# A gated convolution and two MLPs: VectorE's share per unit, block 2's softmax and convolution, and the order inside Y

## The chip, the cores and the metric

The kernel runs on one core of one Trainium2 chip. The metric is the device time of one execution in microseconds (us). The engines are TensorE (PE, with its weight loads listed as PEld), VectorE (DVE), ScalarE (ACT), GpSimd (POOL) and SyncE (SP), which issues the DMAs.

## What is computed

```python
# x: 2 x 4096 x 192, weight_gen: 2 x 4096 x 8 heads x 7 taps; 8192 tokens in all
w = softmax(weight_gen, axis=-1)
out = causal convolution of x with 7 taps, weights w per token and head   # 8192 x 192
xn = out / sqrt(mean(out * out) + 1e-6) * rms_g
g = xn @ w_gate                      # 192 x 1536
x = (g * sigmoid(g) * (xn @ w_val)) @ w_out       # 1536 x 192
h = x @ w_in                         # 192 x 2048
return (h * sigmoid(1.702 * h)) @ w_out2          # 2048 x 192
```

The weight matrices arrive as floats of 64 bits and are split ("decoded") on the chip into a high and a low part; everything else is of 32 bits.

## The kernel before

The 8192 tokens are 16 blocks of 512. Every matmul has a moving operand of 512 tokens and uses 64 of the 128 rows, so they go in pairs, one on the upper rows and one on the lower. Each factor is held as a high part in the reduced format fp32r and a low part, the difference; products are sums of high x high, low x high and high x low.

The work on PE is a list of units. A unit of kind 1, written (1, b, m), makes the gate and value sums of one of 12 column tiles of block b (U1, PSUM tiles pg and pv). A unit of kind 2, (2, b, i), makes two of the 16 column tiles of the second MLP (U2, two tiles ph). Into each unit are woven the down matmuls of earlier units (D1 two units later, D2 one unit later for blocks 0 and 1 and mostly two later else), which add into the long-lived sums a and b. A unit of kind 1 with its down has 14 pairs, one of kind 2 with two has 19. The list begins with 24 units of kind 1, blocks 0 and 1 mixed (unit 6 is (1,1,2), unit 23 is (1,1,11)), then 16 of kind 2, blocks 0 and 1 mixed (24 is (2,0,0), 28 is (2,1,0), 29 is (2,0,4), 36 is (2,1,4)), and unit 40 is (1,2,0). From block 2 on the order repeats: the rest of block b's kind 1, four units of kind 1 of block b + 1, the eight of kind 2 of block b.

Behind the matmuls of a kind-1 unit ACT writes p = silu(pg) (L485), DVE multiplies p by pv (L489), ACT copies p to h (L490), DVE writes l = p - h (L493). In kind 2 ACT makes two silus for each tile, h and p (L506, L507), and DVE l (L513). The PSUM pool of pg, pv and ph has four buffers, so a unit's two tiles are those of two units before: PE's first pair of unit i + 2, which writes both, waits until DVE's p (or ACT's silu) of unit i has read them.

Y(b) (L526), behind the unit with block b's last D1, turns the sums a and b of the first MLP into the inputs of the second: ACT copies two halves of b into yt crosswise (L537, L538) and a into yh (L539); DVE adds b to yt (L540), writes yl = a - yh (L541); ACT copies yt to ysh (L542); DVE writes ysl = yt - ysh (L543).

Weights come in 34 pieces of 384 columns, loaded three ahead. A piece is decoded by one multiply on ACT (x1, L95), five DVE steps (L99, L103, L107, L111, L117) and one or two ACT casts (x6, L122); `piece_steps` runs these for three pieces at once, so that DVE's five steps stand together. Softmax and convolution (softmax_ops, conv_ops) are DVE steps too, but for the exp (ACT, L188, which needs another ACT table than silu), the squares (ACT, L273), the inverse root (POOL, L278 and L280) and half of the scaling (`sc`, DVE L284, ACT L287). In blocks 0 to 4 PE transposes the result.

Every engine runs its instructions in the order in which they are written. A small planner sets that order: stream 0 holds the piece steps and stream 1 softmax and convolution steps, each with a cost and the unit by which it must be done. `share(k, i)` gives the credit that stream k gets in unit i to meet the tightest due unit, and `some` spends it, half ahead of `second` (p and h) and half between `second` and `third` (l); up to unit (1,1,2) both halves stand behind. `ex_at` is the unit at whose head the exp is written, `xt_at` the unit in which a block's transposes are. When a PSUM bank goes from matmuls of the upper rows to matmuls of the lower, a word from POOL (`handed`, L395) stands between.

Of the kernel before, what the change touches and what calls it, by code (L numbers as in the profile page):

```python
# [9 lines left out]
F32 = mybir.dt.float32  # L10
# [8 lines left out]
P = 128  # L19
# [23 lines left out]
def gated_conv_mlp(ctx: ExitStack, tc: tile.TileContext, xp, wg, w1, wo1, w2, wo2, g, out):  # L43
# [174 lines left out]
    def conv_ops(b):  # L218
# [64 lines left out]
        def sc(j):  # L283
            nc.vector.tensor_scalar_mul(out=xr[:, j, 0:D], in0=acc_of[j], scalar1=ri[:, j:j + 1])  # L284
            if b >= TURN:
                return
            nc.scalar.mul(out=xr[:, j, D:2 * P], in_=acc_of[j][:, P:D], mul=ri[:, j:j + 1])  # L287
        for j in range(T):
            ops.append((230, lambda j=j: sc(j)))
        xrow[b] = xr  # L290
# [235 lines left out]
    def Y(b):  # L526
        N = BLOCKS[b] * P
        pa, pb = acc1.pop(b)
        g = "0" if b in (0, NB - 1) else ""
        W = N if g else NM  # L530
        h = ytp.tile([P, W], F32R, tag="yh" + g, name=f"yh{b}")
        l = ytp.tile([P, W], F32R, tag="yl" + g, name=f"yl{b}")
        sh = ytp.tile([P, W], F32R, tag="ysh" + g, name=f"ysh{b}")
        sl = ytp.tile([P, W], F32R, tag="ysl" + g, name=f"ysl{b}")
        t = zp.tile([P, NM], F32, tag="zb", name=f"yt{b}")

        nc.scalar.copy(t[0:DR, :N], pb[DR:P, :N])  # L537
        nc.scalar.copy(t[DR:P, :N], pb[0:DR, :N])  # L538
        nc.scalar.copy(h[:, :N], pa[:, :N])  # L539
        nc.vector.tensor_tensor(out=t[:, :N], in0=t[:, :N], in1=pb[:, :N], op=ALU.add)  # L540
        nc.vector.tensor_tensor(out=l[:, :N], in0=pa[:, :N], in1=h[:, :N].bitcast(F32), op=ALU.subtract)  # L541
        nc.scalar.copy(sh[:, :N], t[:, :N])  # L542
        nc.vector.tensor_tensor(out=sl[:, :N], in0=t[:, :N], in1=sh[:, :N].bitcast(F32), op=ALU.subtract)  # L543
        yT[b] = (h, l, sh, sl)

    def Z(b, own=None):
        N = BLOCKS[b] * P
# [44 lines left out]
        xt_at[b] = pos[1, b - 1, M1 - 8 if b >= TURN else M1 - 2]  # L592
    xt_by_pos = {v: k for k, v in xt_at.items()}
    splits = {}
    group_of = {b0: gi for gi, (b0, b1) in enumerate(GROUPS)}


    at = [0.0]
    for kind, b, m in units:
        at.append(at[-1] + (14 if kind == 1 else 19) * 0.454 * BLOCKS[b] * P)  # L600


    need = []
# [49 lines left out]
    def share(k, i):  # L653

        total, rate = 0.0, 0.0
        for end, c, _ in streams[k]:
            total += c
            rate = max(rate, total / max(1.0, at[min(end, len(units))] - at[i]))
        return rate * (at[i + 1] - at[i])

    def some(amounts):
        for k, a in enumerate(amounts):
# [16 lines left out]
    with ExitStack() as order:  # L679
# [42 lines left out]
        run(conv1[TAPS + 2:])  # L722
        sm[2] = softmax_load(2)
        for p, _ in need[1:]:
            add_work(0, max(0, p - LOOK), [(2150, piece_steps)])
        nxt = 2
        ex_hook = None
        start_at = pos[1, 1, 2]
        soft = {}
        for i, u in enumerate(units):  # L730
            kind, b, m = u
            if (kind, b, m) == (1, 2, 0):
                early.close()
                late = ctx.enter_context(tc.tile_pool(name="late", bufs=6))
                parts.append((late, late))
                squares.append(ctx.enter_context(tc.tile_pool(name="squares", bufs=1)))
# [13 lines left out]
            if i == start_at:  # L750
                if nxt < 4:
                    load_x(nxt)
                end = xt_at[nxt]
                gi = group_of.get(nxt)
                if gi in soft:
                    add_work(1, end - 2, soft.pop(gi) + conv_ops(nxt))
                elif gi is not None and gi >= 2:
                    pr, ex_hook, post_ops = softmax_ops(gi, sm[gi])
                    ex_at = i + 4 if gi == 2 else pos[2, nxt - 2, 2]
                    add_work(1, ex_at, pr)  # L760
                else:
                    gi = group_of.get(nxt + 1)
                    if gi is not None and gi >= 4:
                        pr, ex_hook, soft[gi] = softmax_ops(gi, sm[gi])
                        ex_at = pos[2, nxt - 2, 2]
                        add_work(1, ex_at, pr)
                    add_work(1, end - 2, conv_ops(nxt))
                gi = group_of.get(nxt + (1 if nxt < 4 else 2))
                if gi is not None and gi >= 2 and gi not in sm:
                    sm[gi] = softmax_load(gi)  # L770
# [9 lines left out]
                downs.append(d)  # L780
                after += [f] if f else []
            second, third = (U1 if kind == 1 else U2)(b, m, lambda *ups: matmuls(ups, downs, kind == 2 and b < 2))
            todo = [share(k, i) / 2 for k in (0, 1)]
            if i == 0:
                split = transpose_x(1)
                split(dves=False)
                second()
                split(acts=False)
                third()
                some(todo)  # L790
                some(todo)
            elif i < pos[1, 1, 2]:
                second()
                some(todo)
                third()
                some(todo)
            else:
                some(todo)
                second()
                some(todo)  # L800
                third()
# [60 lines left out]
```

## Time and profile before

| | us |
|---|---|
| median of three runs | 1241.3 (1240.44 to 1241.46) |
| profiled execution | 1240.54 |
| its span | 1238.6 |

The span runs from the first to the last instruction of the profiled execution; 1.9 us lie around it. A row of a timeline has the start, the duration, the engine and line, the operation with its output and inputs, and in brackets the idle time of the engine ahead of it with what ended that. Durations of neighbours overlap a little, so the distance of two starts is the cost in a queue. PE and PEld are one engine: weight loads run beside the matmul before them.

### The profile page before, as it was taken

How to read it: one execution, taken by the hardware profiler on the slowest of the kernel's cores; microseconds unless marked ns; L12 is line 12 of the kernel's file. 1: busy time of each engine (PE TensorE's matmuls, PEld its weight loads, DVE VectorE, ACT ScalarE, POOL GpSimd, SP SyncE). 2: the span in 40 equal slices, each digit the busy share in tenths (PEclk: the TensorE clock that was granted, in tenths of full speed). 3: DMA queues.
4: the chain of work that ended last, by engine and by line, in shares of the span. 5: the costliest groups of instructions: out<-in, count | busy, mean ns of one | idle time of the engine just before them, and what ended most of it. 6: DMA issues, size and time to landing. Idle time of an engine off the chain costs nothing.

```text
span 1238.6 us, 26868 instructions
## 1 busy us (share of the span) xinstructions
PE 1215.7 (98%) x10324; PEld 1100.3 (89%) x10324; DVE 773.1 (62%) x1296; ACT 650.2 (52%) x1279; POOL 32.3 (3%) x53
## 2 busy tenths in 40 slices
PE   5999999999999999999999999999999999999998
PEld 3776999988888999999999989999899998888897
DVE  8989847576657475665747557475664746545432
ACT  4666664555646445454564545446454554544553
POOL 4000000000000000000000000000000000000000
PEclk9999999999999999999999999999999999999999
DMA  5865411001101000110001001001100011000000
GB/s 187 274 182 185 133 57 46 2 1 58 33 16 48 7 25 33 42 34 11 21 33 31 33 16 59 7 26 33 31 33 11 22 33 31 1 15 18 1 14 13
DMA packets 33855, 57.51 MB, mean 46 GB/s; under 512 B 7744, under 2 KB 19392, under 8 KB 33728
## 3 DMA queue, kind: packets, MB, share of 16 engines
q1 hardware_dynamic: 33728, 55.80, 14.5%
q8 instruction: 81, 1.33, 0.4%
q14 instruction: 46, 0.38, 0.1%
HBM read 43.71 MB, written 6.29 MB: 40 GB/s over the span
## 4 chain that ended last, share of the span: by engine, by line
PE 90%; DVE 7%; ACT 2%; issue 1%; DMA 0%; POOL 0%; DVEq 0%; POOLq 0%; ACTq 0%
PE a L380 24%; PE ph L380 21%; PE b L380 16%; PE pv L380 14%; PE pg L380 14%; DVE p L489 1%; DVE l L493 1%; DVE xr L229 1%; DVE dec_a L107 1%; ACT h L490 0%; DVE w L117 0%; DVE dec_s L99 0%; DVE dec_s L111 0%; DVE o L117 0%; DVE acc L262 0%
## 5 line engine op out<-in xcount | busy, mean ns | idle before, releaser
L380 PE MATMUL a<-h,o 64*128 64x512 f32 x1788 | 517.0, 391 | 0.0
L380 PEld LDWEIGHTS a<-h,o 64*128 64x128 f32 x1788 | 326.7, 184 | 14.2
L513 DVE TENSOR_TENSOR l<-p,h 128x512 fp32r<-128x512 f32 x256 | 176.1, 691 | 235.2 <-ACT p L507 233.6
L380 PE MATMUL b<-l,o 64*128 64x512 f32 x896 | 311.2, 393 | 0.1
L380 PE MATMUL a<-l,o 64*128 64x512 f32 x894 | 310.0, 392 | 1.0 <-DVE l L513 0.8
L380 PE MATMUL b<-h,o 64*128 64x512 f32 x896 | 310.4, 392 | 0.0
L506 ACT ACTIVATE h<-ph 128x512 fp32r<-128x512 f32 x256 | 153.9, 601 | 208.5 <-PE ph L380 199.9
L380 PE MATMUL pv<-xh,w 64*128 64x512 f32 x768 | 241.9, 394 | 1.6 <-DVE p L489 1.1
L380 PE MATMUL pg<-xh,w 64*128 64x512 f32 x768 | 242.0, 393 | 1.2 <-ACT w L122 1.2
L380 PE MATMUL ph<-yh,w 64*128 64x512 f32 x1024 | 234.4, 392 | 1.6 <-DVE p L489 1.4
L490 ACT CAST h<-p 128x512 fp32r<-128x512 f32 x192 | 119.4, 622 | 186.3 <-DVE p L489 186.3
L485 ACT ACTIVATE p<-pg 128x512 f32<-128x512 f32 x192 | 114.6, 597 | 164.3 <-PE pg L380 163.7
L489 DVE TENSOR_TENSOR p<-p,pv 128x512 f32<-128x512 f32 x192 | 131.6, 685 | 104.1 <-PE a L380 72.3
L493 DVE TENSOR_TENSOR l<-p,h 128x512 fp32r<-128x512 f32 x192 | 132.6, 691 | 82.9 <-ACT h L490 82.6
L380 PEld LDWEIGHTS a<-l,o 64*128 64x128 f32 x894 | 165.1, 185 | 14.3 <-DVE l L513 2.5
L380 PEld LDWEIGHTS b<-l,o 64*128 64x128 f32 x896 | 165.5, 185 | 8.7 <-DVE l L493 0.5
L380 PEld LDWEIGHTS b<-h,o 64*128 64x128 f32 x896 | 163.9, 185 | 7.7 <-POOLq L395 0.5
L380 PEld LDWEIGHTS ph<-yh,w 64*128 64x128 f32 x1024 | 145.3, 185 | 15.1 <-DVE p L489 2.1
L507 ACT ACTIVATE p<-ph 128x512 f32<-128x512 f32 x256 | 153.9, 601 | 0.0
L380 PEld LDWEIGHTS pv<-xh,w 64*128 64x128 f32 x768 | 140.8, 185 | 14.3 <-DVE p L489 3.8
L380 PE MATMUL ph<-yl,w 64*128 64x512 f32 x512 | 151.2, 391 | 0.0
L380 PE MATMUL pv<-xl,w 64*128 64x512 f32 x384 | 150.5, 392 | 0.0
(117 smaller groups left out, 2098.2 us busy)
## 6 DMA issues: line engine op xcount, KB each, us to landing
x<-in_xp SPq DMA_DIRECT2D x15, 960.0 KB, 4.8
st<-in_w SPq DMA_DIRECT2D x20, 384.0 KB, 4.0
zt<-in_w SPq DMA_DIRECT2D x20, 384.0 KB, 3.4
st<-in_wo SPq DMA_DIRECT2D x14, 384.0 KB, 3.9
zt<-in_wo SPq DMA_DIRECT2D x14, 384.0 KB, 3.4
out_z<-za SPq DMA_DIRECT2D x16, 256.0 KB, 2.2
xl<-raw SPq DMA_DIRECT2D x176, 16.0 KB, 1.8
xsl<-raw SPq DMA_DIRECT2D x176, 16.0 KB, 1.8
```

The source lines that it names most:

```text
L107: nc.vector.scalar_tensor_tensor(out=ai, in0=ai, scalar=3, in1=t["s"], op0=ALU.logical_shift_left, op1=ALU.bitwise_or)
L229: eng.tensor_tensor(out=dst.rearrange("p (q g) -> p q g", g=GRP), in0=x[:, (k + j0) * D:(k + j1) * D].rearrange("p (q g) -> p q g", g=GRP) ...
L380: ins = nc.tensor.matmul(ps[:, :N], w[rows], x[rows, :N], start=start, stop=stop)
L485: nc.scalar.activation(out=p[:, :N], in_=pg[:, :N], func=AF.Silu)
L489: nc.vector.tensor_tensor(out=p[:, :N], in0=p[:, :N], in1=pv[:, :N], op=ALU.mult)
L490: nc.scalar.copy(h[:, :N], p[:, :N])
L493: nc.vector.tensor_tensor(out=l[:, :N], in0=p[:, :N], in1=h[:, :N].bitcast(F32), op=ALU.subtract)
L506: nc.scalar.activation(out=h[:, :N], in_=ps[j][:, :N], func=AF.Silu, scale=SIG)
L507: nc.scalar.activation(out=p[:, :N], in_=ps[j][:, :N], func=AF.Silu, scale=SIG)
L513: nc.vector.tensor_tensor(out=l[:, :N], in0=p[:, :N], in1=h[:, :N].bitcast(F32), op=ALU.subtract)
```

## The change

Six edits. In `sc`, blocks 0 and 1 scale the columns on ACT in another order than on DVE, so that the two work on different PSUM banks. In unit 0 one more step is written at the end, the ACT casts of the next piece. A new function `room` replaces `share` up to block 2: as long as pieces are left, a unit gets as much piece work as DVE has time left by the planner's costs (0.88 of what stays after 1290, and after 1400 more in the units around the Y of blocks 0 and 1), and stream 1 gets nothing; a piece costs 1780 there, 2150 before. `start_at` for block 2 moves from unit 6 to unit 24, and its exp from four units behind that to five. Y is split in two functions, `first` (yh, yl) and `last` (ysh, ysl): for blocks 0 and 1 both are written a unit later, and for the others `first` stands ahead of the yt add and `last` behind it.

```diff
--- before.py
+++ after.py
@@ -284,7 +284,8 @@
             nc.vector.tensor_scalar_mul(out=xr[:, j, 0:D], in0=acc_of[j], scalar1=ri[:, j:j + 1])
             if b >= TURN:
                 return
-            nc.scalar.mul(out=xr[:, j, D:2 * P], in_=acc_of[j][:, P:D], mul=ri[:, j:j + 1])
+            i = (j + T // 2) % T if b < 2 else j
+            nc.scalar.mul(out=xr[:, i, D:2 * P], in_=acc_of[i][:, P:D], mul=ri[:, i:i + 1])
         for j in range(T):
             ops.append((230, lambda j=j: sc(j)))
         xrow[b] = xr
@@ -536,12 +537,22 @@
 
         nc.scalar.copy(t[0:DR, :N], pb[DR:P, :N])
         nc.scalar.copy(t[DR:P, :N], pb[0:DR, :N])
-        nc.scalar.copy(h[:, :N], pa[:, :N])
+        yT[b] = (h, l, sh, sl)
+
+        def first():
+            nc.scalar.copy(h[:, :N], pa[:, :N])
+            nc.vector.tensor_tensor(out=l[:, :N], in0=pa[:, :N], in1=h[:, :N].bitcast(F32), op=ALU.subtract)
+
+        def last():
+            nc.scalar.copy(sh[:, :N], t[:, :N])
+            nc.vector.tensor_tensor(out=sl[:, :N], in0=t[:, :N], in1=sh[:, :N].bitcast(F32), op=ALU.subtract)
+        if b > 1:
+            first()
         nc.vector.tensor_tensor(out=t[:, :N], in0=t[:, :N], in1=pb[:, :N], op=ALU.add)
-        nc.vector.tensor_tensor(out=l[:, :N], in0=pa[:, :N], in1=h[:, :N].bitcast(F32), op=ALU.subtract)
-        nc.scalar.copy(sh[:, :N], t[:, :N])
-        nc.vector.tensor_tensor(out=sl[:, :N], in0=t[:, :N], in1=sh[:, :N].bitcast(F32), op=ALU.subtract)
-        yT[b] = (h, l, sh, sl)
+        if b > 1:
+            last()
+        else:
+            splits[at_unit[0] + 1] = lambda: (first(), last())
 
     def Z(b, own=None):
         N = BLOCKS[b] * P
@@ -592,12 +603,16 @@
         xt_at[b] = pos[1, b - 1, M1 - 8 if b >= TURN else M1 - 2]
     xt_by_pos = {v: k for k, v in xt_at.items()}
     splits = {}
+    at_unit = [0]
     group_of = {b0: gi for gi, (b0, b1) in enumerate(GROUPS)}
 
 
     at = [0.0]
     for kind, b, m in units:
         at.append(at[-1] + (14 if kind == 1 else 19) * 0.454 * BLOCKS[b] * P)
+
+
+    ys = {pos[1, b, M1 - 1] + k for b in range(2) for k in (2, 3)}
 
 
     need = []
@@ -657,6 +672,11 @@
             total += c
             rate = max(rate, total / max(1.0, at[min(end, len(units))] - at[i]))
         return rate * (at[i + 1] - at[i])
+
+    def room(i):
+
+        spare = (at[i + 1] - at[i] - 1290 - (1400 if i in ys else 0)) * 0.88
+        return (spare, 0) if streams[0] else (0, share(1, i))
 
     def some(amounts):
         for k, a in enumerate(amounts):
@@ -722,13 +742,14 @@
         run(conv1[TAPS + 2:])
         sm[2] = softmax_load(2)
         for p, _ in need[1:]:
-            add_work(0, max(0, p - LOOK), [(2150, piece_steps)])
+            add_work(0, max(0, p - LOOK), [(1780, piece_steps)])
         nxt = 2
         ex_hook = None
-        start_at = pos[1, 1, 2]
+        start_at = pos[2, 0, 0]
         soft = {}
         for i, u in enumerate(units):
             kind, b, m = u
+            at_unit[0] = i
             if (kind, b, m) == (1, 2, 0):
                 early.close()
                 late = ctx.enter_context(tc.tile_pool(name="late", bufs=6))
@@ -756,7 +777,7 @@
                     add_work(1, end - 2, soft.pop(gi) + conv_ops(nxt))
                 elif gi is not None and gi >= 2:
                     pr, ex_hook, post_ops = softmax_ops(gi, sm[gi])
-                    ex_at = i + 4 if gi == 2 else pos[2, nxt - 2, 2]
+                    ex_at = i + 5 if gi == 2 else pos[2, nxt - 2, 2]
                     add_work(1, ex_at, pr)
                 else:
                     gi = group_of.get(nxt + 1)
@@ -780,7 +801,7 @@
                 downs.append(d)
                 after += [f] if f else []
             second, third = (U1 if kind == 1 else U2)(b, m, lambda *ups: matmuls(ups, downs, kind == 2 and b < 2))
-            todo = [share(k, i) / 2 for k in (0, 1)]
+            todo = [v / 2 for v in (room(i) if i < pos[1, 2, 0] else (share(0, i), share(1, i)))]
             if i == 0:
                 split = transpose_x(1)
                 split(dves=False)
@@ -789,6 +810,8 @@
                 third()
                 some(todo)
                 some(todo)
+                for f in line[0].pop(0):
+                    f()
             elif i < pos[1, 1, 2]:
                 second()
                 some(todo)
```

DVE, units 11 and 12 of the start (mx and wraw belong to block 2's softmax, dec_, zt and o or w to a weight piece). Before:

```order
L493 TENSOR_TENSOR l1_1_4_985<-p1_1_4_983,h1_1_4_984 128x512
L107 SCALAR_TENSOR_TENSOR dec_a_988<-dec_a_988,dec_s_991 128x384
L99 TENSOR_SCALAR dec_s_1050<-st_939 128x384
L111 TENSOR_SCALAR dec_s_991<-dec_a_988 128x384
L103 TENSOR_SCALAR zt_940<-zt_940 128x384
L117 SCALAR_TENSOR_TENSOR o14_835<-zt_837,dec_s_991 128x2x192
L489 TENSOR_TENSOR p1_0_7_1042<-p1_0_7_1042,pv0_7_1007 128x512
L198 TENSOR_TENSOR wraw2_311<-wraw2_311,mx2_665 128x448
L493 TENSOR_TENSOR l1_0_7_1044<-p1_0_7_1042,h1_0_7_1043 128x512
```

After:

```order
L494 TENSOR_TENSOR l1_1_4_988<-p1_1_4_986,h1_1_4_987 128x512
L107 SCALAR_TENSOR_TENSOR dec_a_991<-dec_a_991,dec_s_994 128x384
L99 TENSOR_SCALAR dec_s_1052<-st_943 128x384
L111 TENSOR_SCALAR dec_s_994<-dec_a_991 128x384
L103 TENSOR_SCALAR zt_944<-zt_944 128x384
L117 SCALAR_TENSOR_TENSOR w1_10_885<-zt_887,dec_s_994 128x384
L490 TENSOR_TENSOR p1_0_7_1043<-p1_0_7_1043,pv0_7_1008 128x512
L494 TENSOR_TENSOR l1_0_7_1045<-p1_0_7_1043,h1_0_7_1044 128x512
```

The softmax step L198 between p and l of unit 12 is gone, and l follows p.

ACT, around the squares of block 2 (L273) and its scaling (L287, after L288). Before, the squares stand ahead of unit 33's silus:

```order
L273 ACTIVATE xr2_885,ss2_887<-acc2_886 128x192 x4
L506 ACTIVATE h2_0_12_2402<-ph0_12_2355 128x512
L507 ACTIVATE p2_0_12_2401<-ph0_12_2355 128x512
L506 ACTIVATE h2_0_13_2407<-ph0_13_2356 128x512
L507 ACTIVATE p2_0_13_2406<-ph0_13_2356 128x512
```

and the scaling stands behind the last silu of unit 35:

```order
L506 ACTIVATE h2_0_14_2526<-ph0_14_2479 128x512
L507 ACTIVATE p2_0_14_2525<-ph0_14_2479 128x512
L506 ACTIVATE h2_0_15_2531<-ph0_15_2480 128x512
L507 ACTIVATE p2_0_15_2530<-ph0_15_2480 128x512
L287 ACTIVATE xr2_885<-acc2_886,ri2_888 128x64 x4
L506 ACTIVATE h2_1_8_2592<-ph1_8_2545 128x512
```

After:

```order
L508 ACTIVATE p2_0_14_2519<-ph0_14_2473 128x512
L507 ACTIVATE h2_0_15_2525<-ph0_15_2474 128x512
L508 ACTIVATE p2_0_15_2524<-ph0_15_2474 128x512
L273 ACTIVATE xr2_2088,ss2_2090<-acc2_2089 128x192 x4
L288 ACTIVATE xr2_2088<-acc2_2089,ri2_2091 128x64 x4
L507 ACTIVATE h2_1_8_2592<-ph1_8_2545 128x512
```

The squares moved behind the last silu of unit 35, with the scaling directly behind them.

DVE, the Y of block 4, with p of (1,5,2) behind it (L229 and xr6 are a convolution step of block 6). Before:

```order
L493 TENSOR_TENSOR l1_5_1_5634<-p1_5_1_5632,h1_5_1_5633 128x512
L540 TENSOR_TENSOR yt4_5644<-yt4_5644,b1_4_4578 128x512
L541 TENSOR_TENSOR yl4_5641<-a1_4_4577,yh4_5640 128x512
L543 TENSOR_TENSOR ysl4_5643<-yt4_5644,ysh4_5642 128x512
L229 TENSOR_TENSOR xr6_5176<-x6_5135,wraw3_2688 128x768
L489 TENSOR_TENSOR p1_5_2_5688<-p1_5_2_5688,pv5_2_5655 128x512
```

After:

```order
L494 TENSOR_TENSOR l1_5_1_5634<-p1_5_1_5632,h1_5_1_5633 128x512
L544 TENSOR_TENSOR yl4_5641<-a1_4_4577,yh4_5640 128x512
L551 TENSOR_TENSOR yt4_5644<-yt4_5644,b1_4_4578 128x512
L548 TENSOR_TENSOR ysl4_5643<-yt4_5644,ysh4_5642 128x512
L229 TENSOR_TENSOR xr6_5176<-x6_5135,wraw3_2688 128x768
L490 TENSOR_TENSOR p1_5_2_5688<-p1_5_2_5688,pv5_2_5655 128x512
```

The yt add moved from ahead of yl to behind it; nothing else moved there.

## Rows read from the trace of the kernel before

**Rows 1.** The page, part 1: busy time, share of the span and instructions
```profile
PE 1215.7 (98%) x10324; PEld 1100.3 (89%) x10324; DVE 773.1 (62%) x1296; ACT 650.2 (52%) x1279; POOL 32.3 (3%) x53
```

**Rows 2.** Table by stage: length, busy (records) by engine, granted clock, DMA
```profile
88.35:132.56 44.21, 41.00 (x323) 31.13 (x321) 40.63 (x85) 29.06 (x61) 0.00 (x0) 1.00 0.59 179
132.56:180.00 47.44, 47.44 (x407) 45.31 (x405) 29.80 (x59) 30.76 (x73) 1.20 (x2) 1.00 0.30 91
```

**Rows 3.** Waits of PE's weight loads, 26 to 135 us: total, times, longest
```profile
PEld pv L380 <- DVE p L489: 3.8, 6, 0.7
...
PEld a L380 <- DVE l L513: 2.5, 4, 0.9
...
PEld ph L380 <- DVE p L489: 2.1, 2, 1.5
...
PEld pv L380 <- POOLq L395: 1.2, 2, 0.7
```

**Rows 4.** Timeline, DVE and PE at the start: start, us, instruction, idle before
```profile
29.32 0.42 DVE L284 TENSOR_SCALAR xr<-bc,ri 128x192 f32<-128x192 f32 x1 [0.38 <-ACT xr L287]
...
38.00 0.50 PE L380 MATMUL pg<-xh,w 64*128 64x512 f32 x1 [1.22 <-ACT w L122]
```

**Rows 5.** Timeline of DVE, units 6 and 17
```profile
53.22 0.68 DVE L489 TENSOR_TENSOR p<-p,pv 128x512 f32<-128x512 f32 x1
...
89.65 0.56 DVE L107 SCALAR_TENSOR_TENSOR dec_a<-dec_a,dec_s 128x384 int32<-128x384 int32 x1
...
92.77 0.69 DVE L493 TENSOR_TENSOR l<-p,h 128x512 fp32r<-128x512 f32 x1 [0.69 <-ACT h L490]
...
93.38 0.55 DVE L107 SCALAR_TENSOR_TENSOR dec_a<-dec_a,dec_s 128x384 int32<-128x384 int32 x1
```

**Rows 6.** Timeline of PE, first matmul of unit 18
```profile
88.35 0.40 PE L380 MATMUL pg<-xh,w 64*128 64x512 f32 x1
```

**Rows 7.** Timeline of ACT: exp of softmax 2, and unit 30's first silu
```profile
62.98 1.28 ACT L188 ACT_TABLE_LOAD   x1
...
66.17 0.60 ACT L485 ACTIVATE p<-pg 128x512 f32<-128x512 f32 x1
...
144.30 0.60 ACT L506 ACTIVATE h<-ph 128x512 fp32r<-128x512 f32 x1 [1.53 <-PE ph L380]
```

**Rows 8.** Near unit 36: ACT, PE, table by stage of L273 alone, POOL
```profile
167.95 0.62 ACT L507 ACTIVATE p<-ph 128x512 f32<-128x512 f32 x1
...
168.08 0.74 PE L380 MATMUL ph<-yh,w 64*128 64x512 f32 x4
...
156.00:157.60 1.60, 1.50 (x8) 1.00 0.00 0
...
162.70 0.20 POOL L278 TENSOR_SCALAR ss<-ss 128x4 f32<-128x4 f32 x1 [139.28 <-ACT h L506]
...
162.98 1.01 POOL L280 TENSOR_TENSOR ri<-ss,half 128x4 f32<-128x4 f32 x1
```

**Rows 9.** Timeline of DVE, block 4's Y and the steps behind it
```profile
385.98 0.69 DVE L540 TENSOR_TENSOR yt<-yt,b 128x512 f32<-128x512 f32 x1 [0.51 <-ACT yt L538]
386.60 0.69 DVE L541 TENSOR_TENSOR yl<-a,yh 128x512 fp32r<-128x512 f32 x1
387.36 0.69 DVE L543 TENSOR_TENSOR ysl<-yt,ysh 128x512 fp32r<-128x512 f32 x1
387.97 0.95 DVE L229 TENSOR_TENSOR xr<-x,wraw 128x768 f32<-128x768 f32 x1
388.84 0.68 DVE L489 TENSOR_TENSOR p<-p,pv 128x512 f32<-128x512 f32 x1
```

**Rows 10.** Timeline of ACT, block 4's Y
```profile
385.98 0.59 ACT L539 CAST yh<-a 128x512 fp32r<-128x512 f32 x1
386.71 0.62 ACT L542 CAST ysh<-yt 128x512 fp32r<-128x512 f32 x1
```

**Rows 11.** Timeline of PE, first matmuls of block 4's kind 2
```profile
389.70 0.63 PE L380 MATMUL ph<-yh,w 64*128 64x512 f32 x4
```

## The prediction

> **What bounds the kernel now.** I read the page's line of engines first: PE is busy 98% of the span, VectorE (DVE) 62%, ScalarE (ACT) 52% [rows 1]. PE is the bound as a whole, so only time in which PE waits can be won. The table by stage then says where that is. From 132.56 to 180 us PE issued 407 half-array matmuls in 47.44 us, 203.5 pairs at 0.233 us each. From 88.35 to 132.56 us, ten units, it had 160 pairs to do, 37.3 us at that pace, and took 44.21. So 6.9 us are lost there, with DVE busy 40.63 of the 44.21 [rows 2]. The waits of PE's weight loads up to 135 us name what it waited for: DVE's product p (L489) 3.8 and 2.1 us, DVE's low part l (L513) 2.5 us, and a word from POOL (L395) 1.2 us [rows 3]. At the pace of 0.233 a kind-1 unit (14 pairs) is 3.26 us of PE and a kind-2 unit (19 pairs) 4.42 us. After that PE runs nearly without a gap for 1100 us, and what matters there is how little any wait would have to grow to show.
>
> **The start (A).** In blocks 0 and 1 the scaling step alternates DVE and ACT on the same PSUM bank; DVE's waits for ACT there, of which one row shows 0.38, are four [rows 4], 1.5 us together. With ACT on the other bank pair they go, and I take 1.4 of DVE time; the transposes, and with them PE's first matmul, come about 0.4 earlier. The second edit is the w1_2 cast (L122) ahead of the second silu: the matmul at 38.00 waited 1.22 for it [rows 4]. 0.4 + 1.22, and 0.2 for the DVE lead in the units between: A = **-1.8**, between -1.2 and -2.2.
>
> **Units 6 to 18, decoding (B).** Before, a unit had one decoded piece and, between p and l, often a softmax or convolution step. Now it has the piece, p and l, with nothing between p and l. What that costs stands in one cycle of before: from L107 at 89.65 to L107 at 93.38 are 3.73 us, in it l's wait of 0.69 for ACT's h [rows 5]. 3.73 is more than PE's 3.26, so DVE sets the pace. The p of unit 6, at 53.22 before [rows 5], comes 1.4 earlier, and 0.53 less for the softmax step that stood ahead of it: 51.3. Ten cycles on, p of unit 16 is at 51.3 + 37.3 = 88.6 and ends at 89.3. PE's second matmul of unit 18 reuses the bank that this p reads; PE starts that unit at 89.4, at 88.35 before [rows 6]. From 1.8 early to 1.0 late: B = **+2.8**. If ACT's h came soon enough to fill the 0.69, the cycle would be 3.04 and B about 0; a conv step in the gap costs no more than 3.8, so its other end is +3.5. I take the cycle that the row shows.
>
> **Units 18 to 28 (C).** These are the ten units that lost 6.9 us: to the softmax and convolution steps of block 2 beside the pieces, and to the Y of blocks 0 and 1. In the new order units 17 to 20 carry the piece between p and l (1.75 + 2 x 0.60 = 2.95 us, below 3.26; the 1.75 of a piece is 92.77 - 89.65 less p and the 0.69 [rows 5]). What stays late is l2_0_1 of unit 24, behind two pieces of 1.75 each: a stall of about 2.1 in unit 25, and 0.3 ahead of it at that unit's bank, which p of unit 23 gives up after a piece. C = -6.9 + 2.4 = **-4.5**, between -3 and -6.
>
> **Units 28 to 30 (D).** The exp of softmax 2 now stands ahead of the two silus of unit 29. From the first table load to the silu behind the second it took 62.98 to 66.17 = 3.19 us; ACT is idle for 1.53 ahead of a unit's first silu [rows 7]. The uncovered 1.7, less what the four-buffer PSUM pool lends, leaves about 1.3. In unit 28 the piece o26 waits on DVE for its multiply on ACT (L95), behind the unit's silus, and l2_1_1 behind it: about 1.4. D = **+2.7**, between 0 and +4. On this row the Trainium skill, page "ScalarE: Activation LUTs", section "What ACT_TABLE_LOAD costs", says otherwise: a switch is 1283 ns of load plus about 1380 ns of drain, 2.66 us, so the pair would be 5.3 us besides the exp, and the sum 2.7 us more. Two loads of 1.28 and an exp fill the 3.19 here with no room for a drain, so the trace disagrees and the sum goes by the row.
>
> **Unit 36 (E).** The convolution of block 2 now ends in the unit before its transposes. Its squares (ACT L273, 1.5 us), the root on POOL (0.20 and 1.01, 1.3 with the gap) and the scaling follow at once. The squares stand behind unit 35's last silu, which before ended 0.5 after unit 36's first matmul [rows 8]. So squares to S + 2.0, root to S + 3.3, S being that first matmul. Behind the root in POOL's queue stand the words for unit 36's row hand-overs, for which PE waits at its sixth pair, S + 1.4; before, the squares were done at 157.6 and the root began at 162.7 [rows 8], with time to spare on both sides. That is a stall of 1.9 to 2.0, and 0.4 for l behind three scalings on DVE: E = **+2.4**, between 0 (if the words are not held) and +3.
>
> The load of x2 moves from the early units to unit 24: 0.98 MB is 5.5 us at the 179 GB/s that DMA moved there before, 0.59 busy [rows 2]. The pieces are loaded three ahead, some 11 us, which covers it; without that cover it would cost up to 2. I put it at 0. The early sum is -1.8 + 2.8 - 4.5 + 2.7 + 2.4 = **+1.6**, with bounds of about -3 and +5.
>
> **Y of every later block (F).** This part decides. For blocks from 2 on, Y now writes yl ahead of the yt add; DVE works in order. Before, in block 4: yt add 385.98 (it waited 0.51 for ACT's yt copy), yl 386.60, ysl 387.36, a conv step 387.97, p 388.84, end 389.52. ACT copied yh from 385.98 to 386.57 and began ysh at 386.71 [rows 9, 10]. Now yl comes first and needs yh: it cannot start before 386.60, where it already was. The yt add moves to 387.21, ysh on ACT (0.73 after the add, as before) to 387.94, ysl (0.65 behind that) to 388.59, and the conv step and p come 1.23 later; p ends at 390.75. DVE idles 1.1 ahead of yl instead of 0.5, and a second time while ACT makes ysh.
>
> PE's first pair of kind 2 began at 389.70 [rows 11], 0.18 behind p's end; I take 0.05 of it, an estimate, for the release, so 0.13 were to spare. It writes the two banks that this p and its silu read (four PSUM buffers, two per unit, two units apart). PE would start it at 390.80: 1.10 lost. Eight blocks (4, 6, 7, 9 to 13) have the conv step between ysl and p in the new order, as here, and had 0.10 to 0.15 to spare. In five (2, 3, 5, 8, 14) p follows ysl at once, 0.87 earlier by the conv step's pitch, so 1.0 is to spare and 0.23 lost. Block 15 has no such unit behind it. F = 8 x 1.10 + 5 x 0.23 = **+10.0**. If the spare were 1.2 or more F would be 0; if the delay spread into the next unit's l, another 0.3 a block, +14. I take the row's value, since it is the pattern of every one of these blocks.
>
> **Sum.** 1240.5 (the profiled execution's own time) + 1.6 + 10.0 = 1252.1. The median of before is 0.8 above that execution: 1252.9 against the median.
>
> **The rivals.** *Early gain kept, Y as computed*: A and C come whole, and B, D and E at half, since each is an overlap that I put together from rows of different units: 1240.5 - 6.3 + 4.0 + 10.0 = 1248.2, about 1249 against the median. For it: PE's lead over DVE in units 6 to 10 may last longer than I think. Against it: the 3.73 cycle is read, not guessed.
>
> *The Y swap is covered* (the other side, not slower): PE does not need p at its first kind-2 pair, or has work queued past it. It decides from a spare of 1.23 us, where I read 0.13. Then F = 0; the bank rule would not bind in B either, and what is left is -1.8 - 4.5 + 2.7 + 2.4 = -1.2: 1239.3, about 1240 against the median. For it: no wait of PE is listed at these places before. Against it: the same bank wait is in rows 3, 2.1 us for ph alone.
>
> *Covered, and the early stalls at half as well*: 1240.5 - 6.3 + 2.6 = 1236.8, about 1237.6. It needs both.
>
> *The change does not do what it says*: a unit gets more decoding than VectorE has time for. That is B, and it is in the forecast.
>
> **How the numbers follow.** The forecast case, both parts as computed (1249.5 to 1256 with the bounds), gets 0.60; early gain kept with slow Y 0.16; Y covered 0.15; covered and early stalls halved 0.09. About 0.2%, 2.5 us, is what a measurement can tell from no change. The first two cases are slower, 0.76; Y covered is 0.12 the same and 0.03 faster, the last case is faster: faster 0.12, same 0.12. The range leaves out the last case and the lower half of the covered one, and a little of the top: 1240 to 1256.5.
>
> **What would show it.** In the changed trace, yl, yt and ysl of block 4 in that order with p about 1.2 later behind them, and PE's ph weight loads waiting for DVE p at every block, eight long waits near 1.1 and five near 0.2. In the first 190 us: no wait for w at 38 us, DVE busy 9 tenths to 110 us, one wait near 2 us in unit 25, and one on POOL in unit 36. PE's rate after the last transposes unchanged and no wait at kind-2 units would refute F; PE at unit 28 earlier by much more than 3.5 us, or later, would refute B or C. A stall of another kind in each block would make the prediction right for the wrong reason.

## The result: slower by 1.3%, a little more than the range held

The changed kernel takes 1257.53 us in the median (1256.98 to 1258.36, four runs) where the kernel before takes 1241.38: a ratio of 1.013, 95% interval [1.0113, 1.0148]. The forecast was 1252.9, with a range up to 1256.5. The direction and the decisive part were right; the time was 4.6 us short. The profiled execution took 1258.36, with a span of 1255.5 (before: 1238.6).

The page of the changed kernel, its line of engines (part 1) and DVE's line by slices (part 2):

```profile
PE 1224.8 (98%) x10324; PEld 1149.9 (92%) x10324; DVE 773.9 (62%) x1296; ACT 651.7 (52%) x1279; POOL 32.1 (3%) x53
...
DVE  8987867566657475665646557375664646545432
```

PE's share is what it was [rows 1]; its busy time has grown by 9 us, although the matmuls are the same 10324. Nothing in these lines tells where 17 us went. The waits of PE's weight loads do (us in total, times, longest), here from 26 to 200 us and then from 200 us on:

```profile
PEld a L381 <- DVE l L514: 8.0, 10, 2.2
PEld pv L381 <- DVE p L490: 5.0, 8, 0.6
...
PEld a L381 <- ACT xr L273: 0.9, 1, 0.9
```

```profile
PEld ph L381 <- DVE p L490: 11.5, 12, 1.4
```

From 200 us on the kernel before shows no wait of this kind at all; now there are twelve, 11.5 us.

The Y of block 4 in the changed kernel, DVE, ACT and then PE, against [rows 9 to 11]:

```profile
390.41 0.69 DVE L494 TENSOR_TENSOR l<-p,h 128x512 fp32r<-128x512 f32 x1 [0.69 <-ACT h L491]
...
392.22 0.69 DVE L544 TENSOR_TENSOR yl<-a,yh 128x512 fp32r<-128x512 f32 x1 [1.11 <-ACT yh L543]
392.83 0.68 DVE L551 TENSOR_TENSOR yt<-yt,b 128x512 f32<-128x512 f32 x1
394.25 0.69 DVE L548 TENSOR_TENSOR ysl<-yt,ysh 128x512 fp32r<-128x512 f32 x1 [0.74 <-ACT ysh L547]
394.86 0.95 DVE L229 TENSOR_TENSOR xr<-x,wraw 128x768 f32<-128x768 f32 x1
395.73 0.68 DVE L490 TENSOR_TENSOR p<-p,pv 128x512 f32<-128x512 f32 x1
```

```profile
391.60 0.59 ACT L543 CAST yh<-a 128x512 fp32r<-128x512 f32 x1
393.59 0.62 ACT L547 CAST ysh<-yt 128x512 fp32r<-128x512 f32 x1 [1.41 <-DVE yt L551]
```

```profile
395.29 0.40 PE L381 MATMUL ph<-yh,w 64*128 64x512 f32 x1
396.46 0.72 PE L381 MATMUL ph<-yh,w 64*128 64x512 f32 x3 [0.78 <-DVE p L490]
```

The l ahead of it in the kernel before:

```profile
384.78 0.69 DVE L493 TENSOR_TENSOR l<-p,h 128x512 fp32r<-128x512 f32 x1 [0.69 <-ACT h L490]
```

yl waits 1.11 us for ACT's yh, ysl 0.74 for ysh. From l (390.41) to p (395.73) are 5.32 us, before 4.06 (384.78 to 388.84): 1.26 more, where I had 1.23. PE starts one matmul of the first pair at 395.29; the other, at 396.46, follows p's end at 396.41.

### The profile page after: what moved, and what is told of

The parts are those of the page before. It is cut to its first block, busy times and chain, and to the rows that moved or that the text cites. A ratio compares the mean times of both kernels' runs of the same rounds, so it can differ in the third digit from the quotient of the medians.

```text
span 1255.5 us, 26881 instructions
## 1 busy us (share of the span) xinstructions
PE 1224.8 (98%) x10324; PEld 1149.9 (92%) x10324; DVE 773.9 (62%) x1296; ACT 651.7 (52%) x1279; POOL 32.1 (3%) x53
## 4 chain that ended last, share of the span: by engine, by line
PE 92%; DVE 6%; ACT 1%; issue 1%; POOL 0%; DMA 0%; DVEq 0%; POOLq 0%
PE a L381 24%; PE ph L381 21%; PE pg L381 16%; PE b L381 15%; PE pv L381 15%; DVE p L490 1%; DVE xr L229 1%; DVE l L494 1%; ACT h L491 1%; DVE dec_a L107 0%; DVE w L117 0%; DVE l L514 0%; DVE acc L262 0%; DVE o L117 0%; DVE dec_s L99 0%
## 5 line engine op out<-in xcount | busy, mean ns | idle before, releaser
L381 PE MATMUL ph<-yh,w 64*128 64x512 f32 x1024 | 245.5, 395 | 6.6 <-DVE p L490 6.6
L381 PEld LDWEIGHTS ph<-yh,w 64*128 64x128 f32 x1024 | 148.0, 185 | 22.7 <-DVE p L490 11.5
L381 PE MATMUL ph<-yl,w 64*128 64x512 f32 x512 | 158.5, 393 | 0.0
L381 PE MATMUL pg<-xl,w 64*128 64x512 f32 x384 | 150.6, 392 | 0.0
```

The costliest lines, as they stand in the source:

```text
L381: ins = nc.tensor.matmul(ps[:, :N], w[rows], x[rows, :N], start=start, stop=stop)
```

## Where the time went

The start of a unit's first matmul in the two profiled executions, changed less before, splits the 16.9 us between their spans by the terms of the prediction:

| up to | difference there | term, measured | predicted |
|---|---|---|---|
| unit 8 | -1.65 | A -1.65 | -1.8 |
| unit 18 | +0.15 | B +1.8 | +2.8 |
| unit 28 | -2.06 | C -2.2 | -4.5 |
| unit 33 | +0.92 | D +3.0 | +2.7 |
| unit 38 | +3.62 | E +2.7 | +2.4 |
| unit 42 | +4.53 | not foreseen +0.9 | 0 |
| end | +16.9 | F +12.4 | +10.0 |

In F, eight blocks lose 1.03 to 1.21 (8.8 in all), each in its first kind-2 unit, and five 0.19 to 0.43 (1.4), there or shortly before. Twelve further steps of 0.07 to 0.17, three units later, make 1.55, and steps too small to place 0.6.

C has a cause of its own. The table by stage of the changed kernel around unit 25 (length, busy us and records of PE, PEld, DVE, ACT, POOL, granted clock, DMA share, GB/s):

```profile
116.00:117.00 1.00, 0.00 (x0) 0.00 (x0) 1.00 (x3) 0.64 (x2) 0.00 (x0) 1.00 1.05 419
117.00:118.00 1.00, 0.62 (x4) 0.57 (x6) 0.32 (x1) 0.00 (x0) 0.00 (x0) 0.89 1.03 396
118.00:119.00 1.00, 1.00 (x8) 0.73 (x6) 0.00 (x0) 0.00 (x0) 0.00 (x0) 0.50 1.01 402
119.00:120.00 1.00, 1.00 (x8) 0.82 (x6) 0.00 (x0) 0.40 (x1) 0.00 (x0) 0.50 1.07 387
120.00:121.00 1.00, 1.00 (x6) 0.80 (x6) 0.02 (x1) 1.00 (x4) 0.00 (x0) 0.50 0.59 237
121.00:122.00 1.00, 1.00 (x10) 0.80 (x8) 1.00 (x2) 0.98 (x3) 0.00 (x0) 0.91 0.05 18
```

PE issues nothing from 116 to 117 us, waiting for l2_0_1 (the longest of the waits for l above, 2.2 us), and then the granted clock is 0.50, the level of 1.2 GHz, for three whole microseconds and parts of two. (1 - 0.89 + 3 x 0.50 + 1 - 0.91) x 2 = 3.4 us at half speed, 1.7 us lost. The unit's loss is 4.0, where I had 2.4.

## The experiments

Each kernel is compared with the kernel before on the same chip.

**Y's old order in the changed kernel.**

```diff
         if b > 1:
-            first()
+            nc.scalar.copy(h[:, :N], pa[:, :N])
         nc.vector.tensor_tensor(out=t[:, :N], in0=t[:, :N], in1=pb[:, :N], op=ALU.add)
         if b > 1:
+            nc.vector.tensor_tensor(out=l[:, :N], in0=pa[:, :N], in1=h[:, :N].bitcast(F32), op=ALU.subtract)
             last()
```

> The changed kernel with one thing undone: in Y of blocks 2 to 15 the yt add again stands ahead of yl on DVE. Theory (the swap costs 1.1 us in eight blocks and about 0.2 in five, and what follows from the later phase of PE's two halves some 0.14 in thirteen): the 12.4 us that were lost behind 200 us come back, time about 1245 us, PE's ph loads no longer wait for DVE p in the blocks, and the small steps four units on are gone too. Rival (the late loss comes from the other order of the planner's steps behind block 3, or from the shifted start): the time stays within 3 us of 1257.

Measured: 1245.56 us (1244.03 to 1246.56), ratio 1.0028 [1.0018, 1.0037], 12.0 below the changed kernel, and 12.4 when each median is taken against that of the kernel before on its own chip. PE's ph loads wait for no p behind 200 us, and the small steps three units later are gone with the large ones. F is this one swap, all of it.

**The swap alone in the kernel before.**

```diff
+        ls = lambda: nc.vector.tensor_tensor(out=l[:, :N], in0=pa[:, :N], in1=h[:, :N].bitcast(F32), op=ALU.subtract)
+        if b > 1:
+            ls()
         nc.vector.tensor_tensor(out=t[:, :N], in0=t[:, :N], in1=pb[:, :N], op=ALU.add)
-        nc.vector.tensor_tensor(out=l[:, :N], in0=pa[:, :N], in1=h[:, :N].bitcast(F32), op=ALU.subtract)
+        if b < 2:
+            ls()
```

> The kernel before with only the swap in Y of blocks 2 to 15: yl ahead of the yt add. Theory (the swap alone makes the late loss): 1241.3 + 10 to 13 = 1251 to 1254 us, with nine stalls near 1.1 (block 5 has its convolution step between ysl and p in this order, so it joins the eight) and four near 0.2. Rival (the loss needs the changed start): below 1244 us.

Measured: 1253.98 us (1253.22 to 1254.19), ratio 1.0096 [1.0081, 1.0111]: 12.1 above the kernel before. Waits from 200 us on:

```profile
PEld ph L380 <- DVE p L489: 12.6, 12, 1.4
```

Nine blocks lose 0.97 to 1.20, block 5 now among them, as its convolution step stands between ysl and p in this order. So the price follows the step that stands there, and the swap needs nothing else of the change.

**The clock in unit 25.** From here on Y has its old order. In unit 24 both l stand ahead of the second piece:

```diff
+            elif (kind, b, m) == (2, 0, 0):
+                some(todo)
+                second()
+                third()
+                some(todo)
             else:
```

> As e1_y_back, and in unit 24 the second l of DVE (l2_0_1) stands ahead of the second decoded piece, so that PE's wait for it in unit 25 shrinks by the 1.75 us of a piece. Theory (the stall of 2.2 us let TensorE's clock fall to 1.2 GHz for about 3 us, which costs another 1.5 to 1.8): the stall shrinks to about 0.5, the granted clock stays at 1.00 from 112 to 124 us, and 3.3 to 3.6 us are won against e1_y_back. Rival (the extra loss there comes from something else, for example from the 400 GB/s of DMA in these microseconds): only the 1.75 us of the piece are won, and the granted clock still falls.

Measured: 1242.86 us (1241.96 to 1243.61), ratio 1.0007 [0.9998, 1.0016], 2.7 below e1_y_back. The same stretch, with DMA as busy:

```profile
116.00:117.00 1.00, 1.00 (x12) 0.82 (x10) 0.65 (x2) 0.59 (x2) 0.00 (x0) 1.00 1.03 393
...
118.00:119.00 1.00, 1.00 (x11) 0.82 (x10) 1.00 (x4) 0.96 (x3) 0.00 (x0) 1.00 0.90 283
...
120.00:121.00 1.00, 0.80 (x8) 0.56 (x7) 0.86 (x2) 0.85 (x2) 0.00 (x0) 1.00 0.95 215
```

The loss of unit 25 falls from 4.00 to 0.77, by 3.2, of which the piece's 1.75 explain about half; the clock stays at 1.00. Some 0.3 of it is given back a unit later; the 2.9 left agree with the 2.7 of the medians.

**The load of block 2's x, early again.**

```diff
+            if (kind, b, m) == (1, 1, 2):
+                load_x(2)
...
-                if nxt < 4:
+                if nxt == 3:
                     load_x(nxt)
```

> As e1_y_back, with the load of block 2's x issued in unit 6 again, as in the kernel before, where the change issues it in unit 24. Theory (its place costs nothing; the loss in unit 25 is the wait for l and the clock): within 0.5 us of e1_y_back, and the granted clock falls again near 118 us. Rival (the load's 400 GB/s at 114 to 120 us make the extra loss of unit 25): 1.5 to 2 us are won against e1_y_back, with no fall of the clock.

Measured: 1244.84 us (1243.57 to 1246.99), ratio 1.0026 [1.0016, 1.0035], against 1245.56 of e1_y_back in the same session: 0.7 apart, where I had 0.5, with intervals that overlap. In the trace the clock falls here too (0.77 at 118 to 120 us, 0.50 at 120 to 122), so a fall does not need the load. Not every execution has one: every trace of this case has at least 3.4 us at 0.50 near its start, and four of the ten executions here have a mean granted clock of 0.998, which leaves at most 6.2 us at half speed, less than the start and a fall of 3.4 us need. They are the four shortest, 1243.57 to 1244.41. No execution of e1_y_back shows 0.998; whether the load makes a fall likelier is open.

**Squares and root a unit apart** (on e3_l_ahead, as the next two).

```diff
-                    add_work(1, xt_at[nxt] - 2, post_ops + conv_ops(nxt))
+                    ops = post_ops + conv_ops(nxt)
+                    if nxt == 2:
+                        ops, tail = ops[:-5], ops[-5:]
+                        splits[xt_at[2] - 3] = lambda: run(tail)
+                    add_work(1, xt_at[nxt] - (3 if nxt == 2 else 2), ops)
```

> As e3_l_ahead, with block 2's convolution due one unit sooner, its squares in unit 34 and the root and the scaling written at the end of unit 35 (in the change the squares stand behind unit 35's silus and the root at once behind them). Theory (the words for unit 36's row hand-overs wait on POOL behind a root that waits for the squares): the 2.1 us in unit 36 and 0.3 around it are gone, 2.1 to 2.5 us won against e3_l_ahead, no wait of PE for POOL near 172 us. Rival (PE waits there for DVE or ACT work that the four scalings push back): less than 0.7 us won.

Measured: 1239.85 us (1239.26 to 1241.04), ratio 0.9993 [0.9984, 1.0002], against 1.0007 of e3_l_ahead: 1.7 us by the ratios. The loss of unit 36 falls from 2.12 to 0.02, and that of unit 40, 0.76, which I had not foreseen, to 0.03. It is less than the 2.1 to 2.5 expected, as 1.0 comes back in units 32 to 34, where the convolution is now denser. In the changed kernel the root and the scaling behind it were (POOL, then ACT):

```profile
171.40 0.19 POOL L278 TENSOR_SCALAR ss<-ss 128x4 f32<-128x4 f32 x1 [147.99 <-ACT xr L273]
171.67 1.01 POOL L280 TENSOR_TENSOR ri<-ss,half 128x4 f32<-128x4 f32 x1
```

```profile
172.72 1.06 ACT L288 ACTIVATE xr<-acc,ri 128x64 f32<-128x64 f32 x4 [1.40 <-POOL ri L280]
```

L280 ends at 172.68 and PE's unit 36 had begun at 169.59: S + 3.1, where I had 3.3. But PE's words did not wait for that end. Its weight loads in unit 36:

```profile
171.76 0.18 PEld L381 LDWEIGHTS a<-h,o 64*128 64x128 f32 x1 [0.92 <-ACT xr L273]
...
174.15 0.18 PEld L381 LDWEIGHTS a<-l,o 64*128 64x128 f32 x1 [1.36 <-DVE l L514]
```

PE goes on at 171.76, behind the squares and L278, while L280 still runs: that wait is 0.92. The longer one, 1.36, is for l, which stands on DVE behind scalings that wait for L280's result. The edit moves squares, root and scaling together, so this run takes both waits away and does not tell them apart; the rows do.

**No table loads in unit 29.** Block 2's exp is replaced by a silu, so this kernel leaves out the exponential in the softmax of blocks 2 and 3.

```diff
-            nc.scalar.activation(out=t, in_=t, func=AF.Exp)
+            nc.scalar.activation(out=t, in_=t, func=AF.Exp if gi != 2 else AF.Silu)
```

> As e3_l_ahead, with block 2's exp replaced by a silu, so that the two ACT table loads in unit 29 fall away; the values of blocks 2 and 3 are not the reference's. Theory (part D: the table loads ahead of unit 29's silus make one of the two stalls near 140 us, the other is the piece o26 behind its multiply on ACT): 1.3 to 1.6 us won, the loss in one of units 29 and 30 gone, the other still 1.4. Rival (both stalls come from the same late ACT): 2.5 to 3 us won. By a drain behind each load, as the page of the Trainium skill has it, another 2.7 us would go.

Measured: 1240.6 us (1239.91 to 1242.36), ratio 0.9999 [0.9989, 1.0008], 1.0 below e3_l_ahead by the ratios, where I had 1.3 to 1.6. The loss of unit 30 falls from 1.50 to 0.10, that of unit 29 stays (1.36). In this profile unit 26 loses 0.7 more, waiting for a weight piece, so that the profile shows less than the 1.4. ACT in the changed kernel:

```profile
137.25 1.28 ACT L188 ACT_TABLE_LOAD   x1
140.07 0.58 ACT L188 ACTIVATE wraw<-wraw 128x448 f32<-128x448 f32 x1 [1.54 <-DVE wraw L181]
140.67 1.28 ACT L507 ACT_TABLE_LOAD   x1
141.97 0.60 ACT L507 ACTIVATE h<-ph 128x512 fp32r<-128x512 f32 x1
```

The exp does not wait for its table: it waits 1.54 for DVE's subtraction (L181). Behind the second load the silu starts 0.02 later. The Trainium skill, page "ScalarE: Activation LUTs", section "What ACT_TABLE_LOAD costs", adds 1.38 us of drain to each switch. These rows have no room for it.

**The piece between p and l in units 6 to 16.**

```diff
-            elif i < pos[1, 1, 2]:
+            elif i < pos[1, 0, 10]:
                 second()
                 some(todo)
                 third()
```

> As e3_l_ahead, with the piece of units 6 to 16 written between p and l, where it fills DVE's wait for h, instead of ahead of p. Theory (part B: DVE's cycle of 3.73 us is p, 0.69 of waiting, l, piece; without the wait it is under PE's 3.26): the eight losses of 0.47 in units 11 to 18 are gone, 3.5 to 3.8 us won by unit 20, and 2.5 to 3.8 kept at the end. Rival (DVE has no time over there whatever the order, and PE's gain is given back where DVE is next late, in units 25 to 28): less than 1.2 us kept at the end.

Measured: 1238.19 us (1237.66 to 1239.55), ratio 0.9981 [0.9972, 0.9991], 3.2 below e3_l_ahead by the ratios. DVE in the changed kernel and in this one:

```profile
77.19 0.68 DVE L490 TENSOR_TENSOR p<-p,pv 128x512 f32<-128x512 f32 x1
78.56 0.69 DVE L494 TENSOR_TENSOR l<-p,h 128x512 fp32r<-128x512 f32 x1 [0.69 <-ACT h L491]
79.17 0.55 DVE L107 SCALAR_TENSOR_TENSOR dec_a<-dec_a,dec_s 128x384 int32<-128x384 int32 x1
...
80.91 0.68 DVE L490 TENSOR_TENSOR p<-p,pv 128x512 f32<-128x512 f32 x1
```

```profile
75.91 0.69 DVE L490 TENSOR_TENSOR p<-p,pv 128x512 f32<-128x512 f32 x1 [0.23 <-ACT p L486]
76.52 0.55 DVE L107 SCALAR_TENSOR_TENSOR dec_a<-dec_a,dec_s 128x384 int32<-128x384 int32 x1
...
78.26 0.68 DVE L494 TENSOR_TENSOR l<-p,h 128x512 fp32r<-128x512 f32 x1
79.17 0.69 DVE L490 TENSOR_TENSOR p<-p,pv 128x512 f32<-128x512 f32 x1 [0.23 <-ACT p L486]
```

The cycle was 80.91 - 77.19 = 3.72 with 0.69 of waiting in it; now it is 3.26, PE's own, and DVE waits 0.23 for silu. All eight losses of 0.47 are gone, and nothing is given back.

**The three together.** The edits of e3_l_ahead, e5_root_later and e7_piece_between; no further line changes.

> e3_l_ahead, e5_root_later and e7_piece_between together: Y's old order, l ahead of the piece in unit 24, root a unit behind the squares, the piece between p and l in units 6 to 16. Theory (the terms add, since they lie in different stretches): 1242.9 - 2.3 - 3.2 = 1236 to 1238 us, 4 to 6 us under the kernel before. Rival (gains of the start are given back in units 25 to 31): 1239 to 1241.

Measured: 1236.25 us (1235.4 to 1236.38), ratio 0.9962 [0.9948, 0.9976]: faster than both kernels, by 0.4% against the kernel before. By the ratios it is 5.6 below e3_l_ahead, where 1.7 and 3.2 of the two other edits make 4.9: the terms add.

**Unit 28 as well.**

```diff
-            elif (kind, b, m) == (2, 0, 0):
+            elif (kind, b, m) in ((2, 0, 0), (2, 1, 0)):
```

> As e8_all, and in unit 28 too DVE writes the second l (l2_1_1) ahead of the piece o26, whose DVE steps wait for ACT's multiply behind the unit's silus. Theory (the other half of part D: l behind a piece that waits for ACT makes the 1.4 us of unit 29): 1.2 to 1.4 us won against e8_all, the time near 1235 us, the 1.5 us at the exp stays. Rival (the late piece pushes the next unit's l instead): less than 0.5 us won.

Measured: 1235.32 us (1235.0 to 1236.11), ratio 0.9951 [0.9937, 0.9964], 1.4 below e8_all by the ratios. The loss of unit 29 falls from 1.35 to 0.06, which shows its cause; that of unit 30 grows from 1.52 to 2.20, probably since PE now reaches the late silus sooner.

**The exp in unit 10.** On e9_l_ahead_28, the maximum, subtraction and exp of block 2 written at the head of unit 10.

```diff
+            if (kind, b, m) == (1, 0, 6):
+                pr, ex2, post_ops = softmax_ops(2, sm[2])
+                run(pr)
+                ex2()
```

> As e9_l_ahead_28, with block 2's softmax up to its exp written in unit 10, as early as in the kernel before, where the change has it in unit 29. Theory (with the piece between p and l DVE and PE run about evenly there, and PE's lead over DVE is some 1 us, so that 3.2 us of ACT and 1.2 us of DVE show in part): 1.5 us won in unit 30, 1 to 3 us lost in units 11 to 14, in all between 0.5 us faster and 1.5 us slower than e9_l_ahead_28. Rival (the four PSUM buffers cover it, as in the kernel before, where the exp cost PE nothing): 1.5 us faster.

Measured: 1235.36 us (1235.28 to 1235.98), ratio 0.9952 [0.994, 0.9965], no different. Units 29 and 30 lose nothing, units 11 and 12 lose 0.5 and 1.3. In the kernel before these two units lose nothing behind the same exp; why was not tested.

**x early, on e9_l_ahead_28.** The diff is that of e4_x_early.

> As e9_l_ahead_28, with the load of block 2's x issued in unit 6 as in the kernel before. Theory (in the trace of e9_l_ahead_28 DVE and ACT wait 0.89 and 0.48 us for a weight piece's DMA near 115 us, while DMA moves some 360 GB/s, so the load of x does hold up a piece once nothing else is late there): 0.5 to 1.5 us won against e9_l_ahead_28, no wait for a piece between 110 and 124 us. Rival (the pieces' own loads fill the queues there, with or without x): within 0.4 us, the waits for DMA stay.

Measured: 1236.14 us (1234.85 to 1236.6), ratio 0.9952 [0.9938, 0.9966]: no gain against e9_l_ahead_28. In the trace there is no wait for a piece's DMA, and PE is 1.4 us ahead of e9_l_ahead_28 by unit 29. Whether that is the price of the load is not shown: e8_all, which has the instructions of e9_l_ahead_28 up to unit 28 and loads x as late, has no such wait in its trace, which began 0.9 us later (unit 26 loses 0.47 there, 1.47 in e9_l_ahead_28). Then unit 30 loses 3.54 instead of 2.20. PE's weight loads there, and the granted clock, in e9_l_ahead_28 and in this kernel:

```profile
135.63 0.18 PEld L381 LDWEIGHTS a<-h,o 64*128 64x128 f32 x1 [1.25 <-ACT h L507]
...
136.61 0.18 PEld L381 LDWEIGHTS b<-h,o 64*128 64x128 f32 x1 [0.69 <-ACT h L507]
...
137.83 0.18 PEld L381 LDWEIGHTS a<-l,o 64*128 64x128 f32 x1 [0.47 <-DVE l L514]
```

```profile
136.00:138.00 2.00, 1.73 (x12) 0.84 (x11) 1.38 (x2) 2.00 (x7) 0.00 (x0) 1.00 0.00 0
138.00:140.00 2.00, 2.00 (x18) 1.88 (x20) 1.92 (x4) 1.90 (x4) 0.00 (x0) 1.00 0.03 8
```

```profile
134.30 0.18 PEld L381 LDWEIGHTS a<-h,o 64*128 64x128 f32 x1 [1.23 <-ACT h L507]
...
135.28 0.18 PEld L381 LDWEIGHTS b<-h,o 64*128 64x128 f32 x1 [0.68 <-ACT h L507]
...
136.49 0.18 PEld L381 LDWEIGHTS a<-l,o 64*128 64x128 f32 x1 [0.46 <-DVE l L514]
```

```profile
136.00:138.00 2.00, 1.98 (x13) 1.45 (x11) 1.69 (x4) 1.62 (x5) 0.00 (x0) 0.71 0.00 0
138.00:140.00 2.00, 2.00 (x12) 1.75 (x12) 1.09 (x3) 1.66 (x4) 0.00 (x0) 0.50 0.04 8
```

The same three waits, 1.2, 0.7 and 0.5; the clock stays at 1.00 in one execution and falls to 0.50 in the other. (0.29 + 0.50) x 2 x 2 = 3.2 us at half speed, 1.6 lost: that is where this execution's lead went. The kernel alone does not decide it. Three of the five executions of e11_x_early (1234.85, 1234.95 and 1236.14 us) have a mean granted clock of 0.998 or 0.999, which by the count above leaves no room for a fall; the profiled one has 0.996.

**The softmax steps ahead of the piece in unit 28.**

```diff
             elif (kind, b, m) in ((2, 0, 0), (2, 1, 0)):
                 some(todo)
                 second()
                 third()
+                while b == 1 and streams[1]:
+                    streams[1].popleft()[2]()
                 some(todo)
```

> As e11_x_early, with the two DVE steps of block 2's softmax that stand ahead of the exp (maximum, subtraction) written ahead of the piece o26 in unit 28, so that the exp need not wait for them. Theory (in e11_x_early the exp begins 0.93 us behind its table load, because it waits for DVE's subtraction, and PE's two waits of 1.2 and 0.7 us behind it let TensorE's clock fall to 1.2 GHz at 136 to 140 us): the waits shrink by 0.9 us together, the granted clock stays at 1.00 and 1.5 to 2.5 us are won against e11_x_early, about 1234 us. Rival (the piece o26, now later, holds up the next unit's l, or the clock falls anyway): less than 0.6 us won.

Measured: 1235.56 us (1234.0 to 1235.77), ratio 0.9952 [0.9938, 0.9965]. In the profile it does what was expected: the exp follows its table load at once, PE's first wait is 0.34, the clock stays at 1.00, unit 30 loses 1.31. The median does not show it: two runs lie at 1234.0, three at 1235.6 to 1235.8, and the starts of the profiled executions alone differ by 0.5 us before unit 3. As e11_x_early itself runs without a fall in three of five executions, a fall could hardly be won back in the median.

## Why the prediction was right in part, and the steps that failed

The direction and the mechanism of the largest term held; the sum was too low. Two steps failed, and both priced a wait of PE at its own length: C, which measured 2.3 us more than forecast, and F, 2.4 more. The other differences, B's -1.0 and the 0.9 of unit 40 and its neighbours above all, nearly cancel.

- **F** was the right mechanism at nearly the right size in the large steps: 8.8 for eight blocks (predicted 8.8) and 1.4 for five (1.15). What failed is the step by which such a wait costs nothing later. The prediction names a spread into the next unit's l, 0.3 a block, and leaves it out of its value; another 1.55 in small steps and 0.6 that can't be placed belong to the swap too, since undoing it returns 12.0 to 12.4 us and the swap alone costs 12.1. What makes the small steps was not tested.
- **C** was mis-sized by 2.3 us. The stall of unit 25 came as worked out (2.2 against 2.1), but it was priced at its length. There is no term for the clock, which in [rows 2] stays at 1.00 through the stalls of before; here it fell behind the stall, another 1.7. Most of the rest is one more turn of B's cycle in unit 18 (0.47) and 0.25 in unit 26. The Trainium skill describes the case of long waits for DMA between groups of matmuls on its page "TensorE: Matmul & The Clock Gate", section "HAM oscillation — how this bites in real kernels": behind each the gate slows the array again. The trace agrees that the clock falls behind a wait; this one was for VectorE, and its 2.2 us are shorter than the waits of that example.
- **B** was the right mechanism. The 3.73 us cycle is there (3.72), and filling the gap takes it away. The term was 1.0 too large at unit 18, because PE's lead lasted until unit 11.
- **A and D** came within 0.3. A's size is that of one execution: in the traces of the kernels built on the changed one, which have the same instructions up to there, unit 3 begins anywhere from 35.6 to 36.6 us. D's two halves, the piece behind its multiply and the exp, were each shown by taking one away. For the exp the price was right with some luck: it also waits 1.54 for DVE, so that ACT needs 4.72 us from the first load to the silu, where the prediction had 3.19.
- **E** came within 0.3 by luck. The words were to wait for the root, 1.9 to 2.0 us, and l another 0.4; the rows of unit 36 show 0.92 for the word, which PE has while the root still runs, and 1.36 for l. The unit loses 2.1, and 0.6 in units 33 and 35, not foreseen, make up the 2.7. Another 0.8 in unit 40, also missed, went when the root came sooner; it is nearly all of the 0.9 of units 38 to 42.
- The load of x costs nothing that the runs can tell from noise in the changed kernel, as said. That it costs anything in the later kernels is not shown: the 0.89 us of waiting for a piece in e9_l_ahead_28 stand in its trace and not in that of e8_all, and the medians of e9_l_ahead_28 and e11_x_early do not part.
- The range ended 1 us below the median measured: it had no term for the clock.

## What to carry to other kernels

When two instructions change places on an in-order engine, ask what each waits for: the one with the later input, moved ahead, makes everything behind it wait, and in a loop with 0.1 us to spare the price is paid in every turn. Price a PE stall of 2 us with a possible fall of its clock on top, not at its length. And a low share of busy time on VectorE says little about room in a unit: its queue had 0.69 us of waiting in each cycle, which another order of the same instructions filled. And a trace is one execution: a wait or a fall of the clock worth 1 to 2 us can stand in it and be gone from the next.

## What the runs showed of the hardware

The length of one wait does not settle whether the granted clock falls. In the kernel before PE's loads waited 1.51 us in one piece and the clock stayed at 1.00:

```profile
111.87 0.29 PEld L380 LDWEIGHTS ph<-yh,w 64*128 64x128 f32 x3 [1.51 <-DVE p L489]
```

```profile
108.00:112.00 4.00, 2.64 (x20) 1.65 (x18) 3.46 (x5) 2.11 (x5) 0.00 (x0) 1.00 0.59 197
112.00:114.00 2.00, 2.00 (x18) 1.68 (x20) 1.50 (x4) 1.82 (x4) 0.00 (x0) 1.00 0.00 0
```

In unit 36 of the changed kernel waits of 0.92 and 1.36 us within 3 us left it at 1.00 too. In unit 25 of that kernel 2.2 us were followed by 3.4 us at 1.2 GHz. In e9_l_ahead_28 and e11_x_early the same three waits, 1.2, 0.7 and 0.5, were followed by a fall in one trace and none in the other, and of e4_x_early and of e11_x_early some executions have a fall and others have none. What decides was not found. A fall costs 1.6 to 1.7 us each time it is seen here.
